# An attention and SwiGLU kernel: query loads one batch ahead, and the crossbar transpose at the first gate slot

## The chip, the cores and the metric

One core of a Trainium2 chip runs the kernel. The time is the device time of one execution in microseconds (us), as a median of several runs. The engines are TensorE (PE, with its weight loads as PEld), VectorE (DVE), ScalarE (ACT), GpSimd (POOL) and SyncE (SP). POOL and SP serve here as queues that issue DMAs, and each issues in the order in which the program writes them.

## The reference

Eight batches with eight heads, 576 tokens and 64 columns per head. Each head first pools its keys and values over the tokens into 32 memory slots, then attends to those; the result of all heads is the input of a gated feed-forward block.

```python
def _attn_ref(q, k, v, phi):
    a = np.exp(phi - np.max(phi, axis=2, keepdims=True))
    a = a / (np.sum(a, axis=2, keepdims=True) + 1e-09)
    k_m = np.einsum('bhsm,bhsd->bhmd', a, k)
    v_m = np.einsum('bhsm,bhsd->bhmd', a, v)
    scores = np.matmul(q, k_m.transpose(0, 1, 3, 2)) / np.sqrt(64)
    attn = np.exp(scores - np.max(scores, axis=-1, keepdims=True))
    attn = attn / (np.sum(attn, axis=-1, keepdims=True) + 1e-09)
    return np.matmul(attn, v_m)

def _moe_ref(x, w_gate, w_val, w_out):     # x: 4608 x 512, d_ff 1536
    g = x @ w_gate
    return (g * (1.0 / (1.0 + np.exp(-g))) * (x @ w_val)) @ w_out
```

## The kernel before

Everything is multiplied in bf16. The program is one straight list of instructions, and each engine runs its own part of the list in the written order; a manual schedule keeps that order. Waits between engines are semaphores that the framework sets from the data and from the reuse of buffers.

**Loads.** POOL issues all loads but the first phi: per batch phi (`load_phi`), keys and values into one tile t_kv (`load_k`, `load_v`), and the query t_q (`load_q`). The pool `inp` has two buffers for each of these tiles. So a load waits until the tile of two batches before has been read, and whatever stands behind it on POOL waits too. Since POOL has little else to do, it runs ahead of the code around it until such a wait stops it.

**The query's transpose.** The scores need the query with its 64 columns on the partitions (t_qT). In batches 0 and 1 TensorE makes it (`q_T`); from batch 2 on `load_qT` issues a DMA from SP that transposes t_q through the crossbar (L88). The same SP queue stores the output tiles (L410). t_qT has two buffers.

**One batch.** The exponential of phi (`phi_exp`, ScalarE); the sums over tokens of keys and values and their normalization (`kv_items`, tiles p_kv, t_bk, t_bv); a transpose of these on TensorE into t_kT (`kv_T`); the scores from t_kT and t_qT (`scores`, L274); their exponential; sums over the memory slots on TensorE and the inverse through a logarithm (`z_inv`, tile t_lz); and the normalized weights t_A on VectorE (`norm`, L303). The attention's output is never formed: the pooled values are multiplied with the gate and value weights (`u_round`, L316, tiles p_u, cast into t_U by VectorE or ScalarE; "vv" has both casts on VectorE, "av" one on each). Then each of 24 slots (`gv_slot`) multiplies t_A with t_U into a gate and a value (L349, p_g and p_v), ScalarE takes silu of the gate (L365, t_sg), and VectorE multiplies the two (L372, t_h).

**The output product** (`out_units`, L396, p_oo, from t_h and the output weights) needs two batches for its tiles of 128 tokens. Its products lie on a list, the backlog, and are taken from it to fill TensorE during the next batch: 28 of them between the scores and the first gate, the rest among the gate slots.

**What sets the order in a batch.** After the scores' stretch, written out by hand, `spread` merges several streams with the 24 gate slots: each stream has a list of items and a first and a last slot, and its items are spaced evenly between the two. So `(kvn, 9, 15)` puts the key/value sums of the next batch at slot 10.5 and the making of its t_kT at 13.5, and `(16, 17)` puts the transpose at slot 16.5.

Of the kernel before, what the change touches and what calls it, by code (L numbers as in the profile page):

```python
# [14 lines left out]
def kernel(  # L15
# [21 lines left out]
    B, H, S, D = q.shape  # L37
# [32 lines left out]
    def load_k(b):  # L70
        t = inp.tile([P, 2, H, J * D], BF16, tag="kv", name="t_kv")
        nc.gpsimd.dma_start(out=t[:, 0], in_=k[b].rearrange("h (p j) d -> p h (j d)", p=P))  # L72
        kvs[b] = t

    def load_v(b):
        nc.gpsimd.dma_start(
            out=kvs[b][:, 1], in_=v[b].rearrange("h (p j) d -> p h (j d)", p=P)
        )

    def load_q(b):  # L80
        t = inp.tile([P, H, J * D], BF16, tag="q", name="t_q")
        nc.gpsimd.dma_start(out=t, in_=q[b].rearrange("h (p j) d -> p h (j d)", p=P))  # L82
        qs[b] = t

    def load_qT(b):

        t = att.tile([128, H, 3, P], BF16, tag="qT", name="t_qT")
        nc.sync.dma_start_transpose(  # L88
            out=t.rearrange("p h j t -> p (h j) t"),
            in_=qs[b].rearrange("p h f -> p (h f)"),  # L90
        )
        for i in range(NP):
            qTs[b, i] = t[:, 2 * i:2 * i + 2].rearrange("p h j t -> p h (j t)")
# [48 lines left out]
    def kv_sum(b, p, parts):  # L142

        w0, w1 = parts[0], parts[-1] + 1
        n = (w1 - w0) * D
        for g in range(NG):
            for j in range(J):
                for i in range(NP):
                    nc.tensor.matmul(  # L149
                        p[32 * i:32 * i + 32, n * g:n * (g + 1)],  # L150
                        lhsT=ephis[b][:, j, g, i],
                        rhs=kvs[b][:, w0:w1, 2 * i + g, j * D:(j + 1) * D],
                        start=(j == 0),
                        stop=(j == J - 1),
                        tile_position=(0, 32 * i),
                    )

    def kv_denominators(b, p, o):
        for g in range(NG):
            for j in range(J):  # L160
                nc.tensor.matmul(  # L161
                    p[:, o + g:o + g + 1],
                    lhsT=ephis[b][:, j, g].rearrange("p i m -> p (i m)"),
                    rhs=ones1[0:P, :],
                    start=(j == 0),
                    stop=(j == J - 1),
                )
        r = att.tile([128, NG, 1, 1], FP32, tag="rS", name="t_rS")
        nc.vector.reciprocal(
            out=r.rearrange("p g a c -> p (g a c)"), in_=p[:, o:o + NG]  # L170
        )
        rSs[b] = r

    def k_norm(b, p):
        bk = att.tile([128, NG, 2, D], BF16, tag="bk", name="t_bk")
        nc.vector.tensor_tensor(
            out=bk,
            in0=p.to_broadcast([128, NG, 2, D]),
            in1=rSs[b].to_broadcast([128, NG, 2, D]),
            op=ALU.mult,  # L180
        )
        bks[b] = bk
# [11 lines left out]
    def kv_T(b, parts):  # L194
        p = ps.tile([128, 3, 128], BF16, tag="s", name="p_T")
        if 0 in parts:
            kTs[b] = att.tile([128, 3, 128], BF16, tag="kT", name="t_kT")
        if 1 in parts:
            nc.tensor.transpose(p[:, 2], bvs.pop(b).rearrange("p g d -> p (g d)"), ident)
        if 0 in parts:  # L200
            bk = bks.pop(b)
            for g in range(NG):
                nc.tensor.transpose(p[:, g], bk[:, g].rearrange("p a d -> p (a d)"), ident)
        lo, hi = (0 if 0 in parts else 2), (3 if 1 in parts else 2)
        nc.vector.tensor_copy(out=kTs[b][:, lo:hi], in_=p[:, lo:hi])
# [17 lines left out]
    def k_items(b):  # L223


        def sums():
            box["k"] = ps.tile([128, NG * D + NG], FP32, tag="s", name="p_kv")
            kv_sum(b, box["k"], (0,))

        def norm():  # L230
            kv_denominators(b, box["k"], NG * D)
            k_norm(b, box["k"][:, 0:NG * D].rearrange("p (g a d) -> p g a d", g=NG, a=1))

        return [sums, norm, lambda: kv_T(b, (0,))]
# [66 lines left out]
    def norm(b, g):  # L301
        a = att.tile([128, 2, HALF], BF16, tag=f"A{g}", name="t_A")
        nc.vector.tensor_tensor(out=a, in0=es.pop((b, g)), in1=lzs.pop((b, g)), op=ALU.mult)  # L303
        atts[b, g] = a
# [83 lines left out]
    def out_units(c, u, eng):  # L388

        mine = {}  # L390

        def unit(jf):
            def run():
                if jf == 0:
                    mine["p"] = ps.tile([128, DM], FP32, tag="o", name="p_oo")
                nc.tensor.matmul(  # L396
                    mine["p"],
                    lhsT=hts[c, jf][:, 128 * u:128 * (u + 1)],
                    rhs=WO[jf],
                    start=(jf == 0),  # L400
                    stop=(jf == NJF - 1),
                )
                if jf == NJF - 1:
                    t_o = work.tile([128, DM], FP32, tag="to", name="t_o")
                    if eng == "a":
                        nc.scalar.copy(out=t_o, in_=mine["p"])
                    else:
                        nc.vector.tensor_copy(out=t_o, in_=mine["p"])  # L408
                    for (r0, n, bb, jj, pp) in token_segments(2 * c * S + 128 * u, 128):
                        nc.sync.dma_start(  # L410
                            out=out_r[bb, jj, pp:pp + n, :], in_=t_o[r0:r0 + n, :]
                        )

            return run

        return [unit(jf) for jf in range(NJF)]

    def out_list(b):
        tiles = range(0, 4) if b % 2 == 0 else range(4, 9)
        res = []  # L420
        for n, u in enumerate(tiles):
            res += out_units(b // 2, u, "v" if n % 4 != 3 else "a")
        return res

    def q_items(b):
        return [lambda i=i: q_T(b, i) for i in range(NP)]

    def u_items(b, evac="av", tags=("ss",)):
        return [
            lambda c=c, which=which: u_round(  # L430
                b, which, c, evac, tags[(2 * c + which) % len(tags)]
            )
            for c in range(NCH)
            for which in range(2)
        ]

    def run(items):
        for x in items:
            x()
# [16 lines left out]
    def warm(n):  # L456

        p = ps.tile([128, DM], FP32, tag="o", name="p_oo")
        for _ in range(n):
            nc.tensor.matmul(p[:, 0:128], lhsT=bones, rhs=bones, start=True, stop=True)  # L460
# [59 lines left out]
    run(k_items(1)[:2])  # L520
    warm(8)
    run(q_items(1)[:2] + k_items(1)[2:] + q_items(1)[2:])
    load_k(2)
    load_v(2)
    load_q(2)
    u1v, u1 = u_items(1, "vv"), u_items(1)
    for g in range(NG):
        scores(1, g)
# [3 lines left out]
    nc.scalar.preload_act_table_set("silu_and_others")  # L532
    run(u1v[:1])
    norm(1, 0)
    run(u1v[1:2])
    norm(1, 1)
    backlog = out_list(0)

    def take(n):
# [5 lines left out]
    for b in range(1, B):  # L545
        last = b + 1 == B
        if b > 1:
            if not last:
                load_phi(b + 1, nc.gpsimd)
                load_k(b + 1)  # L550
                load_v(b + 1)
                load_q(b + 1)
            uw = u_items(b, "vv")
            exp_tables()
            run(take(2))
            for g in range(NG):
                scores(b, g)
            run(take(6) + uw[2:3] + take(4))
            if not last:
                phi_exp(b + 1)  # L560
            for g in range(NG):
                z_inv(b, g)
            nc.scalar.preload_act_table_set("silu_and_others")  # L563
            run(take(4) + uw[3:4] + take(4))
            norm(b, 0)
            norm(b, 1)
            run(take(8))
        rest = take(len(backlog)) if last else take(len(backlog) - 28)
        g = gv_slots(b)
        streams = [(g, 0, 24), (rest, 0, 24)]  # L570
        if b == 1:
            streams += [(u1[2:4], 1, 6), (u1[4:], 8, 14)]
        else:
            streams += [(u_items(b)[4:], 1, 8)]
        if not last:
            kvn = kv_items(b + 1)
            streams += [
                (kvn, 12, 17) if b == 1 else (kvn, 9, 15),
                ([lambda: load_qT(b + 1)], 16, 17),
                (u_items(b + 1)[:2], 18, 24),  # L580
            ]
        spread(*streams)
        flush_mul()
        backlog += out_list(b)
# [31 lines left out]
```

## Time and profile before

| | |
|---|---|
| Time, median of 3 runs | 292.21 us (290.81 to 294.08) |
| Time of the profiled execution | 294.86 us |
| Its span, first to last instruction | 293.0 us |
| TensorE busy | 254.7 us, 87% of the span |
| ScalarE, VectorE busy | 168.6 us, 165.9 us |
| GpSimd busy | 36.0 us |
| DMA: loads by POOL's queue, by SP's queue | 23.01 MB, 13.57 MB |

A matmul's end in the trace is modelled, and matmuls overlap, so a busy TensorE is not one at its peak. A row of a timeline gives start, duration, engine, line and operation, and in brackets the idle time of the engine before it and what ended that. The two queues are q0 (software, issued by POOL) and q1 (hardware, issued by SP).

### The profile page before, as it was taken

How to read it: one execution, taken by the hardware profiler on the slowest of the kernel's cores; microseconds unless marked ns; L12 is line 12 of the kernel's file. 1: busy time of each engine (PE TensorE's matmuls, PEld its weight loads, DVE VectorE, ACT ScalarE, POOL GpSimd, SP SyncE). 2: the span in 40 equal slices, each digit the busy share in tenths (PEclk: the TensorE clock that was granted, in tenths of full speed). 3: DMA queues.
4: the chain of work that ended last, by engine and by line, in shares of the span. 5: the costliest groups of instructions: out<-in, count | busy, mean ns of one | idle time of the engine just before them, and what ended most of it. 6: DMA issues, size and time to landing. Idle time of an engine off the chain costs nothing.

```text
span 293.0 us, 6428 instructions
## 1 busy us (share of the span) xinstructions
PE 254.7 (87%) x2504; PEld 148.6 (51%) x2538; DVE 165.9 (57%) x350; ACT 168.6 (58%) x354; POOL 36.0 (12%) x52
## 2 busy tenths in 40 slices
PE   7587997699439998599959999799999999999993
PEld 7552655356214565146733566346645664466541
DVE  0025785677406767167754677567867776666420
ACT  3148789565437647366557745785697457744300
POOL 8235523202011020100202020100000000000000
PEclk9655999799959999689997999999999999999999
DMA  7999999999979179572797439970512251211233
GB/s 153 225 196 196 219 204 205 207 219 211 209 72 226 36 108 152 90 167 74 92 187 148 124 65 167 104 153 22 115 40 74 54 102 38 72 38 36 73 97 84
DMA packets 48336, 37.00 MB, mean 126 GB/s; under 512 B 15921, under 2 KB 42801, under 8 KB 48305
## 3 DMA queue, kind: packets, MB, share of 16 engines
q0 software_dynamic: 27744, 23.01, 50.5%
q1 hardware_dynamic: 20560, 13.57, 22.6%
q8 instruction: 20, 0.33, 0.5%
q14 instruction: 12, 0.09, 0.1%
HBM read 42.47 MB, written 9.44 MB: 177 GB/s over the span
## 4 chain that ended last, share of the span: by engine, by line
PE 64%; DMA 23%; ACT 6%; DVE 3%; issue 2%; POOL 0%; ACTq 0%; POOLq 0%
PE p_oo L396 25%; DMA t_qT<-t_q 18%; PE p_g L349 15%; PE p_v L349 13%; PE p_u L316 5%; DMA t_q<-in_q_dram 4%; PE p_kv L149 2%; ACT t_lz L297 2%; PE p_g L274 1%; ACT L563 1%; DVE t_U L333 1%; ACT t_lz L298 1%; DVE t_A L303 1%; PE p_q L251 1%; PE p_kv L161 1%
## 5 line engine op out<-in xcount | busy, mean ns | idle before, releaser
L396 PE MATMUL p_oo<-WO,t_h 128*128 128x512 bf16 x398 | 119.6, 393 | 2.1 <-issue 1.0
L372 DVE TENSOR_TENSOR t_h<-t_sg,p_v 128x288 bf16<-128x288 bf16 x192 | 86.6, 454 | 45.7 <-PE p_v L349 42.1
L365 ACT ACTIVATE t_sg<-p_g 128x288 bf16<-128x288 f32 x192 | 79.0, 411 | 56.9 <-PE p_g L349 55.0
L349 PEld LDWEIGHTS <-t_U 128*128 128x128 bf16 x768 | 74.9, 99 | 44.8 <-issue 6.6
L349 PE MATMUL p_g<-t_A,t_U 128*128 128x288 bf16 x384 | 81.0, 292 | 5.9 <-DVE t_A L303 4.0
L349 PE MATMUL p_v<-t_A,t_U 128*128 128x288 bf16 x384 | 79.6, 291 | 0.1
L396 PEld LDWEIGHTS <-t_h 128*128 128x128 bf16 x432 | 41.7, 100 | 39.7 <-issue 15.7
L333 DVE CAST t_U<-p_u 128x512 bf16<-128x512 f32 (+1 forms) x70 | 42.9, 632 | 13.4 <-PE p_u L316 12.7
L408 DVE COPY t_o<-p_oo 128x512 f32<-128x512 f32 x28 | 19.3, 688 | 37.8 <-PE p_oo L396 37.6
L331 ACT CAST t_U<-p_u 128x512 bf16<-128x512 f32 (+1 forms) x38 | 20.1, 530 | 10.9 <-PE p_u L316 10.4
L316 PE MATMUL p_u<-W,t_kT 64*32 64x512 bf16 (+1 forms) x432 | 23.2, 381 | 1.6 <-DVE t_U L333 0.9
L274 PE MATMUL p_g<-t_qT,t_kT 64*32 64x288 bf16 x64 | 5.9, 359 | 17.5 <-DMA t_qT<-t_q 17.0
L135 ACT ACTIVATE t_ephi<-t_phi 96x768 bf16<-96x768 f32 x16 | 12.7, 846 | 9.7 <-DMA t_phi<-in_phi_dram 9.7
L316 PEld LDWEIGHTS <-t_kT 64*32 64x32 bf16 x432 | 6.6, 90 | 20.1 <-issue 19.0
L284 ACT ACTIVATE t_E<-p_g 128x288 bf16<-128x288 f32 x16 | 6.6, 414 | 16.9 <-PE p_v L274 16.9
L72 POOL DMA_DIRECT2D t_kv<-in_k_dram x8 | 6.3, 789 | 65.1 <-PE p_kv L149 47.2
L82 POOL DMA_DIRECT2D t_q<-in_q_dram x8 | 6.2, 773 | 60.0 <-DMA t_qT<-t_q 56.4
L274 PEld LDWEIGHTS <-t_kT 64*32 64x32 bf16 x128 | 1.7, 93 | 22.1 <-DMA t_qT<-t_q 19.0
L303 DVE TENSOR_TENSOR t_A<-t_E,t_lz 128x576 bf16<-128x576 bf16 x16 | 11.5, 750 | 1.0 <-ACT t_lz L298 1.0
L297 ACT ACTIVATE t_lz<-p_g 128x288 f32<-128x288 f32 x16 | 6.4, 402 | 8.9 <-PE p_g L294 8.8
L460 PE MATMUL p_oo<-bones 128*128 128x128 bf16 x98 | 10.0, 295 | 1.5 <-DVE bones L471 1.5
L298 ACT ACTIVATE t_lz<-t_lz 128x576 f32<-128x576 f32 x16 | 10.9, 684 | 0.5
(42 smaller groups left out, 138.4 us busy)
## 6 DMA issues: line engine op xcount, KB each, us to landing
t_kv<-in_k_dram POOLq DMA_DIRECT2D x8, 576.0 KB, 12.6
t_q<-in_q_dram POOLq DMA_DIRECT2D x8, 576.0 KB, 9.9
t_kv<-in_v_dram POOLq DMA_DIRECT2D x8, 576.0 KB, 15.7
out_dram<-t_o SPq DMA_DIRECT2D x24, 192.0 KB, 2.4
t_phi<-in_phi_dram POOLq DMA_DIRECT2D x7, 576.0 KB, 11.1
out_dram<-t_o SPq DMA_DIRECT2D x24, 128.0 KB, 2.4
W<-in_moe_w_gate_dram POOLq DMA_DIRECT2D x6, 256.0 KB, 13.1
W<-in_moe_w_val_dram POOLq DMA_DIRECT2D x6, 256.0 KB, 11.8
```

The source lines that it names most:

```text
L135: nc.scalar.activation(out=t[:, :, g].rearrange("p j i m -> p i j m"), in_=src[:, g], func=AF.Exp)
L297: nc.scalar.activation(out=lz[:, r], in_=p[r][:, 0:HALF], func=AF.Ln)
L298: nc.scalar.activation(out=lz, in_=lz, func=AF.Exp, scale=-1.0)
L303: nc.vector.tensor_tensor(out=a, in0=es.pop((b, g)), in1=lzs.pop((b, g)), op=ALU.mult)
L316: nc.tensor.matmul(p[g][32 * i:32 * i + 32, f0:f1], lhsT=kTs[b][64 * g:64 * g + 64, 2, 32 * i:32 * i + 32], rhs=w, start=True, stop=True, ...
L331: nc.scalar.copy(out=t[:, f0:f1], in_=p[g][:, f0:f1])
L333: nc.vector.tensor_copy(out=t[:, f0:f1], in_=p[g][:, f0:f1])
L349: nc.tensor.matmul(p[:, 0:HALF], lhsT=Us[b, which, c, g][:, 128 * o:128 * (o + 1)], rhs=atts[b, g][:, r], start=(g == 0), stop=(g == NG - 1),)
L365: nc.scalar.activation(out=sg, in_=gate, func=AF.Silu)
L372: nc.vector.tensor_tensor(out=dst, in0=sg, in1=val, op=ALU.mult)
L396: nc.tensor.matmul(mine["p"], lhsT=hts[c, jf][:, 128 * u:128 * (u + 1)], rhs=WO[jf], start=(jf == 0), stop=(jf == NJF - 1),)
L408: nc.vector.tensor_copy(out=t_o, in_=mine["p"])
```

## The change

Query loads move one batch ahead: before batch 1's slots, query 2 is loaded ahead of keys and values 2 and query 3 behind them, and batch b loads query b+2 in place of b+1. The transpose of the next batch's query is written at slot 0 (slot 6 in batch 1) in place of slot 16.5. In batch 1 the key/value sums of batch 2 move from slots 12 to 17 to slots 16 to 22, and the first U rounds of batch 2 from 18 to 24 to 21 to 24. Also in batch 1, the second U round comes behind both normalizations, with one of its casts on ScalarE.

```diff
+    load_q(2)
     load_k(2)
     load_v(2)
-    load_q(2)
+    load_q(3)
...
     run(u1v[:1])
     norm(1, 0)
-    run(u1v[1:2])
     norm(1, 1)
+    run(u1[1:2])
...
                 load_k(b + 1)
                 load_v(b + 1)
-                load_q(b + 1)
+                if b + 2 < B:
+                    load_q(b + 2)
...
             streams += [
-                (kvn, 12, 17) if b == 1 else (kvn, 9, 15),
-                ([lambda: load_qT(b + 1)], 16, 17),
-                (u_items(b + 1)[:2], 18, 24),
+                (kvn, 16, 22) if b == 1 else (kvn, 9, 15),
+                ([lambda: load_qT(b + 1)], 6, 6) if b == 1 else ([lambda: load_qT(b + 1)], 0, 0),
+                (u_items(b + 1)[:2], 21 if b == 1 else 18, 24),
             ]
```

On SP, from its first load on, before. The numbers are the program's buffer numbers: t_qT_1368 is batch 2's, t_qT_1886 batch 3's, and each t_o is one output tile.

```order
L67 DMA t_phi_84<-in_phi_dram 96x8x192
L410 DMA out_0_dram<-t_o_1328 96x512
L410 DMA out_0_dram<-t_o_1328 32x512
L88 DMA_TRANSPOSE t_qT_1368<-t_q_939 128x24x96
L410 DMA out_0_dram<-t_o_1509 64x512 x2
L410 DMA out_0_dram<-t_o_1560 32x512
L410 DMA out_0_dram<-t_o_1560 96x512
L410 DMA out_0_dram<-t_o_1595 96x512
L410 DMA out_0_dram<-t_o_1595 32x512
L410 DMA out_0_dram<-t_o_1722 64x512 x2
L88 DMA_TRANSPOSE t_qT_1886<-t_q_1476 128x24x96
```

The same place on SP after the change, where batch 2's is t_qT_1156 and batch 3's t_qT_1601.

```order
L67 DMA t_phi_84<-in_phi_dram 96x8x192
L88 DMA_TRANSPOSE t_qT_1156<-t_q_936 128x24x96
L410 DMA out_0_dram<-t_o_1265 96x512
L410 DMA out_0_dram<-t_o_1265 32x512
L410 DMA out_0_dram<-t_o_1511 64x512 x2
L410 DMA out_0_dram<-t_o_1562 32x512
L410 DMA out_0_dram<-t_o_1562 96x512
L410 DMA out_0_dram<-t_o_1597 96x512
L410 DMA out_0_dram<-t_o_1597 32x512
L88 DMA_TRANSPOSE t_qT_1601<-t_q_941 128x24x96
L410 DMA out_0_dram<-t_o_1726 64x512 x2
```

Batch 2's transpose now stands ahead of all stores, and batch 3's ahead of one more tile's store than before.

On POOL, from the last weights on, before: keys and values of batch 2, its query, then batch 3's phi, keys, values and query.

```order
L116 DMA WO2_132<-in_moe_w_out_dram 128x4x512
L72 DMA t_kv_936<-in_k_dram 96x8x384
L76 DMA t_kv_936<-in_v_dram 96x8x384
L82 DMA t_q_939<-in_q_dram 96x8x384
L67 DMA t_phi_1471<-in_phi_dram 96x8x192
L72 DMA t_kv_1473<-in_k_dram 96x8x384
L76 DMA t_kv_1473<-in_v_dram 96x8x384
L82 DMA t_q_1476<-in_q_dram 96x8x384
```

The same place on POOL after the change: t_q_936 is batch 2's query, t_q_941 batch 3's and t_q_1478 batch 4's.

```order
L116 DMA WO2_132<-in_moe_w_out_dram 128x4x512
L82 DMA t_q_936<-in_q_dram 96x8x384
L72 DMA t_kv_938<-in_k_dram 96x8x384
L76 DMA t_kv_938<-in_v_dram 96x8x384
L82 DMA t_q_941<-in_q_dram 96x8x384
L67 DMA t_phi_1473<-in_phi_dram 96x8x192
L72 DMA t_kv_1475<-in_k_dram 96x8x384
L76 DMA t_kv_1475<-in_v_dram 96x8x384
L82 DMA t_q_1478<-in_q_dram 96x8x384
```

One query load has come to stand ahead of keys and values 2; from there on the order of kinds is the same, with each query one batch further.

On VectorE, ahead of batch 1's first gate slots, before: casts of the first two U rounds (p_u) and the two normalizations (t_A).

```order
L333 CAST t_U_1048<-p_u0_1038 128x512
L333 CAST t_U_1050<-p_u1_1039 128x512
L303 TENSOR_TENSOR t_A_1052<-t_E_951,t_lz_1023 128x576
L333 CAST t_U_1064<-p_u0_1054 128x512
L333 CAST t_U_1066<-p_u1_1055 128x512
L303 TENSOR_TENSOR t_A_1068<-t_E_964,t_lz_1031 128x576
```

The same place on VectorE after the change.

```order
L333 CAST t_U_1050<-p_u0_1040 128x512
L333 CAST t_U_1052<-p_u1_1041 128x512
L303 TENSOR_TENSOR t_A_1054<-t_E_953,t_lz_1025 128x576
L303 TENSOR_TENSOR t_A_1056<-t_E_966,t_lz_1033 128x576
L333 CAST t_U_1070<-p_u1_1059 128x512
```

The second normalization stands ahead of the second round's cast; the other cast of that round is now on ScalarE, behind its table load.

## Rows read from the trace of the kernel before

**Rows 1.** The page's chain that ended last, by engine and by line.

```profile
PE 64%; DMA 23%; ACT 6%; DVE 3%; issue 2%; POOL 0%; ACTq 0%; POOLq 0%
PE p_oo L396 25%; DMA t_qT<-t_q 18%; PE p_g L349 15%; PE p_v L349 13%; PE p_u L316 5%; DMA t_q<-in_q_dram 4%; PE p_kv L149 2%; ACT t_lz L297 2%; PE p_g L274 1%; ACT L563 1%; DVE t_U L333 1%; ACT t_lz L298 1%; DVE t_A L303 1%; PE p_q L251 1%; PE p_kv L161 1%
```

**Rows 2.** The waits: who waited for what, total us, times, longest.

```profile
POOL t_q L82 <- DMA t_qT<-t_q: 56.4, 4, 16.4
...
PE p_g L274 <- DMA t_qT<-t_q: 17.0, 4, 8.3
```

**Rows 3.** Timeline of TensorE: the first scores of batches 2 to 5.

```profile
85.09 0.42 PE L274 MATMUL p_g<-t_qT,t_kT 64*32 64x288 bf16 x1 [8.28 <-DMA t_qT<-t_q]
...
120.49 0.42 PE L274 MATMUL p_g<-t_qT,t_kT 64*32 64x288 bf16 x1 [3.90 <-DMA t_qT<-t_q]
...
153.95 0.42 PE L274 MATMUL p_g<-t_qT,t_kT 64*32 64x288 bf16 x1 [3.26 <-DMA t_qT<-t_q]
...
186.80 0.29 PE L274 MATMUL p_g<-t_qT,t_kT 64*32 64x288 bf16 x1 [1.58 <-DMA t_qT<-t_q]
```

**Rows 4.** Two transposes in the chain (start, us), then the view of t_qT.

```profile
70.52 14.54 DMA t_qT<-t_q
...
105.01 15.44 DMA t_qT<-t_q
...
L88 SPq DMA_TRANSPOSE t_qT<-t_q x6: 2973/5584/8695, 70.5 to 232.5; - x6
...
DMA to landing us min/median/max: 5.0/11.6/15.4
```

**Rows 5.** DMA queues (packets, MB, share) at 52-54 us, 72-74 (q1), 76-78 (both).

```profile
q0 software_dynamic: 530, 0.40, 129.6%
...
q1 hardware_dynamic: 9, 0.02, 3.6%
...
q0 software_dynamic: 374, 0.28, 89.0%
q1 hardware_dynamic: 376, 0.10, 36.5%
```

**Rows 6.** First scores to first gate, batches 2 to 6; PEclk is third from the end.

```profile
85.09:94.31 9.22, 9.06 (x63) 3.50 (x65) 5.03 (x8) 6.75 (x14) 1.56 (x2) 0.81 0.85 177
120.49:130.50 10.01, 9.68 (x61) 3.63 (x63) 4.45 (x7) 6.74 (x14) 1.56 (x2) 0.71 0.74 144
153.95:162.93 8.98, 8.76 (x62) 3.49 (x64) 5.03 (x8) 6.74 (x14) 1.56 (x2) 0.83 0.84 170
186.80:194.18 7.38, 7.22 (x61) 3.16 (x63) 4.45 (x7) 6.74 (x14) 0.77 (x1) 1.00 0.82 132
214.30:222.14 7.84, 7.79 (x64) 3.34 (x65) 5.35 (x9) 7.53 (x15) 0.00 (x0) 1.00 0.28 69
```

**Rows 7.** DMA issues at 34-36 and 36.5-40 us: us to landing last.

```profile
t_kv<-in_k_dram POOLq DMA_DIRECT2D x1, 576.0 KB, 20.9
...
t_kv<-in_v_dram POOLq DMA_DIRECT2D x1, 576.0 KB, 21.3
```

**Rows 8.** Timeline of POOL: the issues of keys and values 2.

```profile
35.44 0.79 POOL L72 DMA_DIRECT2D t_kv<-in_k_dram  x1 [1.09 <-PE p_u L316]
37.98 0.78 POOL L76 DMA_DIRECT2D t_kv<-in_v_dram  x1 [1.74 <-DMA t_phi<-in_phi_dram]
```

**Rows 9.** TensorE's sums of batch 2; then from the view of p_T.

```profile
66.49 0.85 PE L149 MATMUL p_kv<-t_kv,t_ephi 96*32 96x128 bf16 x48 [0.38 <-ACT t_U L331]
...
PE p_u L316: 0.3, 1
```

**Rows 10.** Timelines of VectorE, ScalarE and TensorE ahead of batch 1's gates.

```profile
52.22 1.28 DVE L333 CAST t_U<-p_u 128x512 bf16<-128x512 f32 x2
...
52.37 1.28 ACT L532 ACT_TABLE_LOAD   x1
...
54.22 0.28 PE L349 MATMUL p_g<-t_A,t_U 128*128 128x288 bf16 x1 [1.58 <-DVE t_A L303]
```

## The prediction

> **What bounds the kernel now.** I read the chain that ended last first: TensorE holds 64% of it, DMA 23%, and the crossbar transpose that makes t_qT 18% [rows 1]. The waits say what of that is an idle TensorE: the scores at L274 wait for t_qT four times, 17.0 us in all, longest 8.3 [rows 2]. The timeline puts these waits at the first scores of batches 2, 3, 4 and 5: 8.28, 3.90, 3.26 and 1.58 us, together 17.02 [rows 3]; batches 6 and 7 have none. The transposes behind the first two were issued at 70.52 and 105.01 and took 14.54 and 15.44 us, while one with the queues empty lands in 5.0 [rows 4].
>
> Why they are slow is in the DMA packets. At 52 to 54 us the software queue, which carries all loads, moves 530 packets in 2 us; at 76 to 78, beside a transpose, it moves 374 and the transpose 376: the two queues share packet by packet [rows 5]. Before, a transpose is issued at slot 16.5 of a batch's 24, just after the key/value sums (slots 9 to 15, 12 to 17 in batch 1) have freed a buffer and so released the next keys and values. As long as there are loads left, it meets them, and only about 6 us of gate slots are left to hide it (TensorE ran out of work at 76.8 after the issue at 70.52).
>
> The idle time costs twice. From the first scores to the first gate, the granted clock averaged 0.81, 0.71 and 0.83 in batches 2, 3 and 4, so part of each stretch ran at the 1.2 GHz level; after the short wait of batch 5, and in batch 6 without one, it was 1.00 [rows 6]. Even and odd batches hold slightly different work here, so I compare 2 and 4 with 6, and 3 with 5: 9.22 - 7.84 = 1.38, 8.98 - 7.84 = 1.14, 10.01 - 7.38 = 2.63, together 5.15 us.
>
> **The transposes of batches 3 to 7** move from slot 16.5 to slot 0. On SP they now stand right behind the stores of the tiles that are copied out as the gates begin, so I expect them to issue about a microsecond after the first gate. From there to the next scores are 20 to 22 us: batch 2's first gate is at 85.09 + 9.22 = 94.31, and batch 3's scores could start at 120.49 - 3.90 = 116.59. Against 22.3 stands a worst landing of 15.44 [rows 4]. The source is there too: query b+1 is loaded behind the landing of transpose b-1, more than a batch before. The four waits fall to nothing: -17.02, with batch 2 included under the condition below. What hides the transposes is the gate slots; if that cover went, up to these 17 us would return. Stores on SP wait behind the transpose instruction (longest 8.7 us on SP [rows 4]); a tile is 12 of the 32 output products spread over 22.3 us, so one comes every 8 us, and there are three output buffers. I cost that at nothing; without that cover a copy would wait for what is left, at most 0.7 us a batch.
>
> **The clock**: without idle TensorE I take back the 5.15. The lower bound is 0, if the clock falls for another reason; the upper is 5.15, since the other stretches already show 1.00.
>
> **Batch 2 is the tight one.** Loads now stand on POOL as query 2, keys 2, values 2, query 3. Query 2 takes the place of keys 2, issued at 35.44 and landed 20.9 later, at 56.3 [rows 7, 8]; keys 2 take values' place (37.98 + 21.3 = 59.3), values 2 the query's, one load later again (62.3). The first transpose stands ahead of every store on SP, and its other waits are for batch 0's t_qT, long done, so it issues when query 2 lands, about 56.3, whatever slot the code names. Beside it the software queue still holds six loads of 3.0 us (the spacing of these landings): 18.0 us. In the same trouble at 70.52 the transpose took 14.54. Its 576 KB go in packets of some 256 bytes (0.10 MB in 376), 2,304 of them; at 376 per 2 us that is 12.3 us, and at 72 to 74 us only 9 had flowed [rows 5], so I add 3.5 for the start: 15.8. So it lands at 71 to 72; batch 2's scores could start at 85.09 - 8.28 = 76.8, 75.8 with the gain below. It holds by about 4 us.
>
> Keys and values 2 are read later, at slot 17.5 instead of 13.25. The old sums ran at 66.49 [rows 9], 12.3 us after the first gate at 54.22 [rows 10], so 0.93 us per slot; the new ones come at 70.4, against values that land at 62.3 plus 1 to 2 for the sharing. No wait. Then t_kT is copied one slot, not four, ahead of the first U round of batch 2, which must wait for the copy. The view of p_T has one such wait, 0.3 us [rows 9]. Bounds 0 to 1.0 (a copy queued behind one multiply); I take +0.3, nearest to the row.
>
> **The U round in batch 1.** VectorE runs two casts, 1.28 us from 52.22, between the two normalizations; the first gate waits 1.58 for the second [rows 10]. Now that second normalization can run when its t_lz is ready, at 52.37 where the table load begins, not at 53.50: 1.1 earlier. But one cast moves to ScalarE behind the 1.28 us table load, so it begins at 53.65 at the earliest, and the first value product and the first silu on ScalarE wait for it. Bounds 0 and -1.1; I take -0.7, as the gate comes 1.1 earlier and the value by somewhat less.
>
> **Sum** on the profiled execution (span 293.0, time 294.86): -17.02 - 5.15 - 0.7 + 0.3 = -22.6, giving 272.3. The median of the three runs shown is 292.21; from there it would be 269.6. If runs differ by these very waits, the first is the better basis; if by anything else, the second. I forecast **271.0**. What is late next is TensorE itself: undisturbed batches show it busy nearly throughout, 7.79 of 7.84 us [rows 6].
>
> **A rule against the clock term.** Batches 2 to 4 show 5.15 us, 1.8% of the span, going with low clocks [rows 6]. The Trainium skill (TensorE: Matmul & The Clock Gate, Part 1, "What's actually happening") says that "the ramp penalty is <1% of a typical kernel span". By that rule, an estimate from the page, at most 2.9 us would return and the sum would be about 274.5. The trace disagrees, so I leave the term whole. Rival C is the mechanism.
>
> **Rivals.**
> A, the forecast: waits and clock both go; 271.0, its own range 268 to 274. Chance 0.68.
>
> B, batch 2's transpose still late: the loads keep more than half of the engines, and the transpose ends only with the software queue. Then 56.3 + 18.0 + 5.0 = 79.3, against 75.8: a wait of 3.5 and a clock loss near batch 4's 1.14. 271.0 + 4.5 = 275.5. For: no transpose shown has met six loads. Against: the one-to-one packets give a fixed pace. 0.16.
>
> C, the clock stays low at the scores although nothing waits (odd batches did most poorly, for no visible reason): 271.0 + 2.6 to 5.15, say 274.5. Against: batches 5 to 7 at 1.00. 0.08.
>
> D, slower: the transposes and query loads close a loop. Transpose b+1 frees the buffer for query b+3, and POOL holds the next phi, keys and values behind that load. One turn is a transpose plus a query load: at the worst landings shown, 15.44 plus 21.3 [rows 4, 7], 36.7 us per two batches, against 57.6 of work (30.1 for an even batch: 7.84 plus 22.3; 27.5 for an odd one, from 186.80 to 214.30 [rows 6]). It decides only above 57.6; at 68 it would add 5.2 per batch, 26 over five, giving 297. 0.03.
>
> E, the change doesn't do what it says: SP reaches the transposes as late as before, because a store ahead waits for its tile. Then 17 us of waits stay: 292. Against: that tile is finished as the gates begin. 0.05.
>
> **How the numbers follow.** A measurement of this kernel tells about 1% from no change, 2.9 us. A, B and C are faster, 0.92; E the same, 0.05; D slower, 0.03. For 8 in 10 I take A's range and B and C: low 267.0 (269.6 less the rest of the U bound and some for the runs' spread), high 277.5 (B on the profiled basis: 272.3 + 4.5, rounded up).
>
> **What would show it.** Right: no wait of L274 for t_qT; granted clock 1.00 from first scores to first gate in batches 2 to 4; that stretch 7.4 (odd) or 7.8 (even); DMA out of the chain after 60 us; the first transpose issued at 56 and landing by 72; later ones landing in 5 to 8 us. Wrong: a wait at batch 2's scores (B); low clock without a wait (C); POOL holding keys past their slot (D); SP issues still late in the batch (E); or TensorE waiting for t_kT at the end of batch 1 by more than a microsecond.

## The result, and the profile after

The changed kernel takes 275.51 us (median of four runs, 272.71 to 276.99); the kernel before took 291.78 beside it (290.81 to 294.08). The ratio is 0.94, with a 95% interval of 0.930 to 0.950: faster, inside the range of 267.0 to 277.5, and 4.5 us above the 271.0 that stood for the likeliest case. The profiled execution is the longest of the four, 276.99 with a span of 275.2, so it is set against the sum's own basis of 272.3. Ratios here and below leave out executions more than 1.5% above the fastest of their kernel; the profiled one is just such a one, but `e2_q_pad`, profiled in an execution of 276.02 that is not left out, shows the same wait and the same granted clock at batch 2 (3.48 us, 0.73) and the same times in batches 3 and 4 (7.50, 7.84).

The page's chain of the changed kernel, by engine and by line, to be read beside [rows 1]:

```profile
PE 70%; DMA 13%; ACT 11%; issue 3%; DVE 1%; POOL 1%; ACTq 0%; POOLq 0%
PE p_oo L396 26%; PE p_g L349 17%; PE p_v L349 15%; DMA t_qT<-t_q 8%; PE p_u L316 5%; DMA t_q<-in_q_dram 4%; ACT t_lz L297 2%; PE p_kv L149 2%; ACT t_ephi L135 2%; ACT t_lz L298 2%; ACT L565 1%; ACT L451 1%; PE p_g L274 1%; ACT t_E L284 1%; PE p_q L251 1%
```

The transpose fell from 18% to 8% and did not leave. The waits say how often it still holds TensorE [rows 2]:

```profile
POOL t_q L82 <- DMA t_qT<-t_q: 93.2, 4, 28.3
...
PE p_g L274 <- DMA t_qT<-t_q: 3.5, 1, 3.5
```

One wait of 3.5 us in place of four with 17.0. In the timeline of TensorE, the first scores of batches 2 to 5 [rows 3]:

```profile
78.88 0.42 PE L274 MATMUL p_g<-t_qT,t_kT 64*32 64x288 bf16 x1 [3.55 <-DMA t_qT<-t_q]
...
111.20 0.29 PE L274 MATMUL p_g<-t_qT,t_kT 64*32 64x288 bf16 x1
...
138.82 0.29 PE L274 MATMUL p_g<-t_qT,t_kT 64*32 64x288 bf16 x1
...
168.87 0.29 PE L274 MATMUL p_g<-t_qT,t_kT 64*32 64x288 bf16 x1
```

Batches 3, 4 and 5 start without a wait; batch 2 waits 3.55. The windows from the first scores to the first gate, in the columns of [rows 6], with batch 2's idle time ahead of them:

```profile
75.33:78.88 3.55, 0.00 (x2) 0.00 (x1) 0.25 (x1) 0.83 (x1) 0.00 (x0) 0.81 0.96 172
78.88:88.98 10.10, 9.77 (x62) 3.69 (x64) 5.03 (x8) 6.74 (x14) 3.07 (x4) 0.73 1.00 183
111.20:118.70 7.50, 7.34 (x63) 3.22 (x63) 4.64 (x8) 7.40 (x15) 0.00 (x0) 1.00 0.51 98
138.82:146.66 7.84, 7.79 (x64) 3.33 (x65) 5.35 (x9) 7.52 (x15) 0.00 (x0) 1.00 0.93 177
168.87:176.37 7.50, 7.34 (x62) 3.24 (x63) 4.65 (x8) 7.39 (x15) 0.00 (x0) 1.00 0.14 39
```

Batches 3 to 5 run at the granted clock of 1.00 and take 7.50, 7.84 and 7.50 us, where they took 10.01, 8.98 and 7.38. Batch 2 is at 0.73 and takes 10.10, more than the 9.22 of before. The transposes, first batch 2's in the chain (start, us), then the view of t_qT [rows 4]:

```profile
55.63 23.20 DMA t_qT<-t_q
```

```profile
DMA to landing us min/median/max: 5.1/6.1/23.2
```

Batch 2's was issued at 55.63, as early as forecast, and landed 23.2 us later, at 78.83. The others land in 5.1 to 8.3. The DMA queues (packets, MB, share) at 62 to 72 us, then at 72 to 74 [rows 5]:

```profile
q0 software_dynamic: 975, 1.20, 91.9%
q1 hardware_dynamic: 982, 0.25, 46.1%
...
q0 software_dynamic: 354, 0.27, 90.4%
q1 hardware_dynamic: 345, 0.09, 38.6%
```

One packet against one holds in both. But at 62 to 72 the transpose gets 98 packets per us, not the 188 of [rows 5], and picks up again to 173 at 72. In the slow stretch a packet of the loads carries 1.20 MB / 975 = 1.23 KB on average, in the fast one 0.76 KB.

Stage by stage the 17.8 us that the span lost are: 1.5 up to batch 2's wait (half of it ahead of batch 1's first gate, where runs differ by about as much); 17.02 - 3.55 = 13.5 of waits; and 2.77 of the clock: 2.51 in batch 3 (10.01 to 7.50) and 1.14 in batch 4 (8.98 to 7.84), less the 0.88 that batch 2 lost (9.22 to 10.10).

### The profile page after: what moved, and what is told of

The parts are those of the page before. It is cut to its first block, busy times and chain, and to the rows that moved or that the text cites. A ratio compares the mean times of both kernels' runs of the same rounds, so it can differ in the third digit from the quotient of the medians.

```text
span 275.2 us, 6425 instructions
## 1 busy us (share of the span) xinstructions
PE 251.8 (91%) x2503; PEld 147.6 (54%) x2538; DVE 165.4 (60%) x349; ACT 168.8 (61%) x355; POOL 35.9 (13%) x52
## 3 DMA queue, kind: packets, MB, share of 16 engines
q1 hardware_dynamic: 20560, 13.57, 23.3%
## 4 chain that ended last, share of the span: by engine, by line
PE 70%; DMA 13%; ACT 11%; issue 3%; DVE 1%; POOL 1%; ACTq 0%; POOLq 0%
PE p_oo L396 26%; PE p_g L349 17%; PE p_v L349 15%; DMA t_qT<-t_q 8%; PE p_u L316 5%; DMA t_q<-in_q_dram 4%; ACT t_lz L297 2%; PE p_kv L149 2%; ACT t_ephi L135 2%; ACT t_lz L298 2%; ACT L565 1%; ACT L451 1%; PE p_g L274 1%; ACT t_E L284 1%; PE p_q L251 1%
## 5 line engine op out<-in xcount | busy, mean ns | idle before, releaser
L396 PE MATMUL p_oo<-WO,t_h 128*128 128x512 bf16 x397 | 117.0, 386 | 2.0 <-issue 0.8
L365 ACT ACTIVATE t_sg<-p_g 128x288 bf16<-128x288 f32 x192 | 78.8, 411 | 55.4 <-PE p_g L349 53.1
L333 DVE CAST t_U<-p_u 128x512 bf16<-128x512 f32 (+1 forms) x69 | 42.3, 631 | 10.8 <-PE p_u L316 10.1
L331 ACT CAST t_U<-p_u 128x512 bf16<-128x512 f32 (+1 forms) x39 | 20.7, 531 | 11.1 <-PE p_u L316 10.6
L316 PE MATMUL p_u<-W,t_kT 64*32 64x512 bf16 (+1 forms) x432 | 23.2, 379 | 1.5 <-DVE t_U L333 0.8
L82 POOL DMA_DIRECT2D t_q<-in_q_dram x8 | 6.2, 774 | 99.9 <-DMA t_qT<-t_q 93.2
L316 PEld LDWEIGHTS <-t_kT 64*32 64x32 bf16 x432 | 6.7, 90 | 19.5 <-issue 18.0
L406 ACT COPY t_o<-p_oo 128x512 f32<-128x512 f32 x8 | 4.7, 586 | 10.8 <-DMA out_dram<-t_o 10.0
L149 PE MATMUL p_kv<-t_kv,t_ephi 96*32 96x128 bf16 (+1 forms) x480 | 7.9, 219 | 2.8 <-DMA t_kv<-in_k_dram 2.8
L460 PEld LDWEIGHTS <-bones 128*128 128x128 bf16 x98 | 9.0, 135 | 1.5 <-DVE bones L471 1.5
```

What stands on the lines that cost most here:

```text
L149: nc.tensor.matmul(p[32 * i:32 * i + 32, n * g:n * (g + 1)], lhsT=ephis[b][:, j, g, i], rhs=kvs[b][:, w0:w1, 2 * i + g, j * D:(j + 1) * D] ...
L316: nc.tensor.matmul(p[g][32 * i:32 * i + 32, f0:f1], lhsT=kTs[b][64 * g:64 * g + 64, 2, 32 * i:32 * i + 32], rhs=w, start=True, stop=True, ...
L331: nc.scalar.copy(out=t[:, f0:f1], in_=p[g][:, f0:f1])
L333: nc.vector.tensor_copy(out=t[:, f0:f1], in_=p[g][:, f0:f1])
L365: nc.scalar.activation(out=sg, in_=gate, func=AF.Silu)
L396: nc.tensor.matmul(mine["p"], lhsT=hts[c, jf][:, 128 * u:128 * (u + 1)], rhs=WO[jf], start=(jf == 0), stop=(jf == NJF - 1),)
```

## The experiments

Each kernel differs from the changed one by the edit shown. Times are medians of four executions. The median of the kernel before, run beside them, was 293.07 (`e1`, `e2`, `e4`, `e5`), 292.70 (`e3`, `e6`, `e7`), 291.68 (`e8`, `e9`) and 293.10 (`e10`).

### Which half took away the waits of batches 3 to 5

The prediction gave the gain to the new slot (S); the rival is the earlier load of the query (L). `e4_slot_old` keeps the loads and puts the transposes back:

```diff
-                ([lambda: load_qT(b + 1)], 6, 6) if b == 1 else ([lambda: load_qT(b + 1)], 0, 0),
+                ([lambda: load_qT(b + 1)], 16, 17),
```

> The changed kernel with the transposes back at slot 16.5, query loads still one batch ahead. Theory S (the slot carries the gain): the transposes meet the next keys and values again, and batches 3 to 5 wait some 2 to 4 us each; with the clock 12 us come back on top of batch 2's, time near 285. Theory L (the loads carry it): a query load that waits for the transpose now stands ahead of the next phi, keys and values, so those cannot start before the transpose has landed; it runs alone, lands in 5 to 6 us inside the 7 us of slots left, and batches 3 to 5 do not wait; only batch 2 waits, 4 to 6 us, time 276 to 278.

271.98 us, ratio 0.9393 (0.9274 to 0.9512), so not slower than the whole change (0.94, 0.930 to 0.950). The timeline of TensorE at batch 2's scores, then of POOL in batch 3:

```profile
76.49 0.29 PE L274 MATMUL p_g<-t_qT,t_kT 64*32 64x288 bf16 x1 [2.58 <-DMA t_qT<-t_q]
```

```profile
101.27 0.77 POOL L82 DMA_DIRECT2D t_q<-in_q_dram  x1 [21.17 <-DMA t_qT<-t_q]
102.03 0.79 POOL L67 DMA_DIRECT2D t_phi<-in_phi_dram  x1
102.80 0.78 POOL L72 DMA_DIRECT2D t_kv<-in_k_dram  x1
```

Batches 3 and 5 to 7 don't wait, batch 4 waits 0.21. The reason stands on POOL: the query load needs the buffer that the transpose is reading, so it waits 21.17 us for it, and phi, keys and values are queued behind it. Batch 3's transpose, issued at 94.86, therefore runs without loads beside it and lands in 5.8 us. The order of the loads alone keeps them out of its way.

`e5_loads_old` keeps the new slots and puts the loads back:

```diff
-    load_q(2)
     load_k(2)
     load_v(2)
-    load_q(3)
+    load_q(2)
...
-                if b + 2 < B:
-                    load_q(b + 2)
+                load_q(b + 1)
```

> The changed kernel with the loads in the old order (keys, values, query of the same batch), transposes still at slot 0 (6 in batch 1). Theory S: batches 3 to 5 do not wait, since the query is there a batch ahead anyway and 20 us of slots are left; landings 5 to 9 us. Theory L: without the early loads the waits of batches 3 to 5 return, some 9 us and the clock, near 285. Batch 2 by both: query 2 lands three microseconds later per load ahead of it, near 62, and the transpose then meets phi, keys, values and query 3, so that it lands near 80 and the scores wait 4 to 6 us; time by theory S 276 to 278.

282.03 us, ratio 0.9751 (0.9617 to 0.9885): slower than the whole change, and whether it gains 2% on the kernel before is not settled. TensorE at batch 2's scores, and the view of t_qT:

```profile
85.08 0.42 PE L274 MATMUL p_g<-t_qT,t_kT 64*32 64x288 bf16 x1 [10.34 <-DMA t_qT<-t_q]
```

```profile
DMA to landing us min/median/max: 5.0/5.4/22.9
```

Batches 3 to 7 don't wait here either. So each half is enough for batches 3 to 5, and the two gains don't add. Batch 2 tells them apart: without the early query its transpose is issued at 62.18 instead of 55.63 and lands at 85.0, a wait of 10.34. What the change gained in batch 2 is the load order's. The early slot gains nothing there: with the old loads the transpose is issued 8.3 us earlier than before and lands at the same 85.0; with the new loads it lands at 78.8 from the new slot, and at 76.4 from the old one (66.08, 10.4 us to landing). Counted from batch 1's first gate, since runs start apart by a microsecond or two, the new slot's landings come at 34.0 us against 32.7 with the old loads, and at 27.2 against 25.9 with the new ones; each is one profiled execution.

### What slows batch 2's transpose: the query's packets?

The first guess was query 3, which the change had put into the queue. `e1_q3_behind` loads it behind phi, keys and values 3:

```diff
-    load_q(3)
...
                     load_q(b + 2)
+                if b == 2:
+                    load_q(3)
```

> The changed kernel with one load moved: query 3 goes behind phi, keys and values 3 instead of ahead of them. Batch 2's transpose still starts beside six loads (keys and values 2; phi, keys, values 3; query 3), but query 3 is now the last of them. Theory P (packet size): the two queues take turns packet by packet, and a query load consists of a few large packets, so beside it the transpose falls to half its pace; without it the pace stays near 376 packets in 2 us, it lands 15 to 18 us after its issue at about 55.6, near 72, the 3.55 us wait at batch 2's scores goes, the clock of that stretch returns to 1.00 and the stretch from 10.0 to about 7.8; time about 5.5 us less than the changed kernel, near 270. Theory W (sum of work): the transpose ends only with the software queue whatever stands in it; it lands near 79 again and the time stays near 275.

272.45 us, ratio 0.9429 (0.9238 to 0.962); the transpose lands in 20.9 us and the wait is 1.55. The large packets did not move with query 3: they now flow at 58 to 64 us, just before phi 3 lands (issued at 41.75, landed at 65.2), while query 3 at the end of the queue goes in small ones. `e2_q_pad` pads the query's tile, so that its rows don't lie end to end:

```diff
-        t = inp.tile([P, H, J * D], BF16, tag="q", name="t_q")
+        t = inp.tile([P, H + 1, J * D], BF16, tag="q", name="t_q")[:, 0:H]
```

> The changed kernel with the query tile one head wider than needed, so that the rows of a query load are no longer one closed block per partition; order of all loads unchanged, one head of each t_q tile is never written or read. Theory P: if that breaks the query's packets into the 768-byte pieces of the other loads (mean packet size of the software queue near 0.75 KB throughout 60 to 74 us, where it was 1.2 KB between 62 and 72), the transpose of batch 2 keeps 376 packets in 2 us and lands near 72; time near 270. If the packets stay large, nothing changes, 275, and this says nothing. Theory W: 275 in both cases, the landing near 79.

276.24 us, ratio 0.9542 (0.9418 to 0.9667); landing in 22.1 us, a wait of 3.48: nothing changed. The guess fell. Phi is the load that remains, and the only one that doesn't cast: f32 in memory and f32 in its tile.

### Phi's packets, or the whole queue?

Rival B of the prediction said that the transpose ends only with the software queue (W). `e6_phi3_first` loads phi 3 ahead of query 2, so that it is through before the transpose:

```diff
+    load_phi(3, nc.gpsimd)
     load_q(2)
...
-                load_phi(b + 1, nc.gpsimd)
+                if b > 2:
+                    load_phi(b + 1, nc.gpsimd)
```

> The changed kernel with the load of phi 3 moved ahead of query 2. The last runs put the slow stretch of batch 2's transpose where phi 3 flows: with phi 3 in its old place behind query 3 at 62 to 71 us, with query 3 put last still at 58 to 64. Theory P2 (the large packets are those of the phi loads, and the transpose gets one 256-byte packet per phi packet): phi 3 now flows before query 2 has landed, so the transpose never meets it; it is issued some 3 us later, near 58.5, keeps 376 packets in 2 us, takes 15 to 17 us, lands near 74.5 and batch 2's scores wait 0 to 0.5 us; time near 270.5. Theory W (it waits for the whole queue): the same six loads less one beside it, 58.5 + 15 + 5 = 78.5, a wait of 3 us, time near 275.

271.23 us, ratio 0.9296 (0.9217 to 0.9375). Batch 2's transpose in the chain, and the queues at 62 to 72 us:

```profile
57.90 17.78 DMA t_qT<-t_q
```

```profile
q0 software_dynamic: 1722, 1.29, 88.9%
q1 hardware_dynamic: 1740, 0.45, 40.8%
```

The loads move as many bytes as before (1.29 MB against 1.20), in 1,722 packets in place of 975, and the transpose gets 1,740 in place of 982. It lands at 75.7 although it starts 2.3 us later. A wait of 2.30 is left, where 0 to 0.5 was expected: the landing came 1.2 us later than expected, and TensorE was there at 73.4, in the changed kernel at 75.3. `e7_phi_pad` was meant to make phi's packets small by padding its tile:

```diff
-        t = inp.tile([P, H, J * M], FP32, tag="phi", name="t_phi")
+        t = inp.tile([P, H, J * M + 8], FP32, tag="phi", name="t_phi")[:, :, 0:J * M]
```

> The changed kernel with the phi tile 32 bytes longer per head and partition, so that the eight heads of a partition are no longer one closed block; order of all instructions unchanged, the added columns are never written or read. Theory P2: the phi loads go in 768-byte packets like the others (mean of the software queue 0.75 KB throughout 60 to 72 us), the transpose of batch 2 keeps 376 packets in 2 us and lands 15 to 17 us after its issue at 55.6, near 71.5; no wait, the stretch after it at clock 1.00 and 7.8 us; time 5.5 us below the changed kernel, near 270. Theory W: the landing stays near 79 and the time near 275. If the packets of phi stay large this says nothing.

276.34 us, ratio 0.9438 (0.9355 to 0.9521), a wait of 5.31. The transpose lands at 78.4, as in the changed kernel; the wait is longer because TensorE is there earlier, at 73.1. Its queues at 62 to 72 us:

```profile
q0 software_dynamic: 1086, 1.27, 91.3%
q1 hardware_dynamic: 1085, 0.28, 44.2%
```

The packets stayed large (1.17 KB on average), so the edit did not make what it should have tested. `e9_phi3_cast` does: phi 3 gets a bf16 tile, and its load casts as the others do and writes half the bytes in all.

```diff
-        t = inp.tile([P, H, J * M], FP32, tag="phi", name="t_phi")
+        if b == 3:
+            t = inp.tile([P, H, J * M], BF16, tag="phib", bufs=1, name="t_phi")
+        else:
+            t = inp.tile([P, H, J * M], FP32, tag="phi", name="t_phi")
```

> The changed kernel with one edit: the tile of phi 3 is bf16 in a buffer of its own, so its load casts as those of query, keys and values do; phi of that one batch is rounded to bf16, and its load writes half the bytes. Nothing moves in any order. P: between 60 and 72 us the software queue shows no packets over about 800 bytes, the pace stays at 185 to 190 per us, the transpose issued near 55.6 lands at 71 to 73, no wait for t_qT at batch 2's scores, granted clock 1.00 from first scores to first gate, 269 to 270.5. N: the transpose lands at 78 to 79 as before, a wait of 3 us or more, 275.

269.62 us, ratio 0.9292 (0.9225 to 0.9359). The queues at 62 to 72 us, and batch 2's first scores (L277 is L274 here, three lines lower):

```profile
q0 software_dynamic: 2083, 1.27, 88.4%
q1 hardware_dynamic: 2080, 0.53, 44.4%
```

```profile
75.99 0.29 PE L277 MATMUL p_g<-t_qT,t_kT 64*32 64x288 bf16 x1
```

No instruction moved in its engine's order, the loads write as many bytes in this stretch (1.27 MB), and only their packets are smaller, 0.61 KB on average. The transpose gets 208 packets per us, more than twice as many, lands in 17.5 us, and the wait is gone. The stretch behind it is at 1.00, 7.84 us.

`e8_phi3_last` puts phi 3 behind keys and values 3:

```diff
-                load_phi(b + 1, nc.gpsimd)
+                if b > 2:
+                    load_phi(b + 1, nc.gpsimd)
                 load_k(b + 1)
                 load_v(b + 1)
+                if b == 2:
+                    load_phi(b + 1, nc.gpsimd)
```

> The changed kernel with one edit: the load of phi 3 stands behind keys and values 3, not ahead of them. The same loads are still queued when batch 2's transpose is issued, but the ones beside it are all loads that cast. P (the transpose gets one packet per packet of its neighbour, and phi's packets are large): the pace stays at 185 to 190 packets per us from 60 us on, so the transpose, issued near 55.6, lands at 71 to 74, and the scores of batch 2 don't wait for t_qT. Phi 3 then lands last, at 79 to 81, some 2 to 3 us after ScalarE wants it, so a part of the gain may go to the waits behind its exponential; 270 to 273. N (what counts is how much is queued, whatever its packets): landing at 78 to 79, a wait of 3 us or more, 275.

272.82 us, the median of six executions, one of which took 413.33; ratio 0.9284 (0.9204 to 0.9364). The queues at 68 to 70 us and at 70 to 72:

```profile
q0 software_dynamic: 378, 0.29, 90.8%
q1 hardware_dynamic: 377, 0.10, 36.3%
...
q0 software_dynamic: 269, 0.36, 92.9%
q1 hardware_dynamic: 271, 0.07, 32.7%
```

The pace was 189 per us up to 70, as expected; then, with the transpose not yet done, packets of 1.34 KB on average appeared, and it fell. The landing took 21.0 us and the wait was 2.40. Phi 3 held ScalarE for 0.30 only. The expected landing was missed because I had phi's packets come behind the transpose; the pace before and after 70 answers to the packets again.

### The U round in batch 1

`e3_u_old` puts the second U round back between the normalizations, with both casts on VectorE:

```diff
     norm(1, 0)
+    run(u1v[1:2])
     norm(1, 1)
-    run(u1[1:2])
```

> The changed kernel with the second U round of batch 1 back ahead of the second normalization, both casts on VectorE. The prediction's term of 0.7 us: the first gate of batch 1 waits about 1.6 us for the second normalization instead of 0.56, and the stretch from the first gate to batch 2's last slot is 0.3 to 1.0 us longer. Since the transpose of batch 2 is the last to come there, a later batch 1 only shortens the wait for it (3.55 to about 2.8), so the time stays at 275 to 276. Rival: the cast on ScalarE costs as much as it saves, and the stretch is as long as in the changed kernel.

274.73 us, ratio 0.9392 (0.9313 to 0.9471), not to be told from the changed kernel. TensorE at the second half of the first gate:

```profile
52.17 0.39 PE L349 MATMUL p_g<-t_A,t_U 128*128 128x288 bf16 x1 [1.58 <-DVE t_A L303]
```

The wait of 1.58 is back; in the changed kernel it is 0.56. That is 1.0 us at this place. From batch 1's first gate to batch 2's scores, without the wait there, TensorE took 24.19 us against 23.71, so half a microsecond of it is left; with batch 2's transpose late (a wait of 3.67 here) none of it shows in the time.

### A better order

`e10_q2_ahead` loads query 2 ahead of the output weights:

```diff
-    for c in range(3):
-        load_wo(c)
...
     load_q(2)
+    for c in range(3):
+        load_wo(c)
     load_k(2)
```

> The changed kernel with one edit: the three loads of the output weights stand behind query 2, not ahead of it. Phi 3 keeps its large packets and its place. Query 2 is issued near 31 in place of 34.7 and lands near 52, so the transpose is issued near 52, 3.6 us earlier than in the changed kernel, and has that much longer beside packets of loads that cast. If the pace beside phi 3's packets is the whole matter, it has done 3.6 x 188 = 680 more of its 2,304 packets before phi's arrive, and lands at 73 to 75: no wait or at most 0.5 us at batch 2's scores, 269.5 to 271. If the transpose can't end before the software queue has emptied, it still lands near 78, with a wait of 3 us, 275. Against it: the last output weights land 3 us later, near 54, and the first output product runs at 52.6 today; at most 1 us for that.

270.21 us, each of four executions between 269.73 and 270.50 (beside 293.10 of before, with no ratio on record; the changed kernel's lie between 272.71 and 276.99). Batch 2's first scores, and the view of t_qT:

```profile
73.91 0.29 PE L274 MATMUL p_g<-t_qT,t_kT 64*32 64x288 bf16 x1
```

```profile
DMA to landing us min/median/max: 5.1/6.1/18.4
```

Query 2 landed at 47.3, the transpose 18.4 us later at 65.7, 8 us before its scores; I had it at 73 to 75. It was through before all but a few of phi 3's packets came (at 66 to 68 us the software queue moved 0.55 MB in 244 packets, 2.3 KB each), and long before the queue was empty: values 3, issued at 50.04, landed 26.8 us later, at 76.8. That speaks against W a second time. The output weights caused no wait. Of the kernels that do not round phi, this has the lowest median, though the 271.23 of `e6_phi3_first` can't be told from it.

## Why the prediction was right and where it failed

**The waits of batches 3 to 5** went, as forecast: 3.90 + 3.26 + 1.58 = 8.74 us. The reason given, the slot, is one of two that suffice (`e4_slot_old`, `e5_loads_old`).

**Batch 2** is the step that failed: "at 376 per 2 us that is 12.3 us ... So it lands at 71 to 72". The issue was right (56.3 against 55.63) and the share of one packet to one was right. The start was nearly right (3.5 allowed; some 44 packets had flowed 4.4 us after the issue), by luck in part: the 9 packets that it was read from [rows 5] carry 0.02 MB, 2 KB each, so they were the output stores', not the transpose's of 256 bytes. The pace was wrong. It was read from a stretch in which the neighbours were loads that cast, with 0.75 KB to a packet, and taken for all six loads. Phi 3 is one of the six; beside it the pace is 98 per us and the transpose takes 23.2 us instead of 15.8. Of these 7.4 us, an estimate from the packet counts puts 4.8 on the pace at 62 to 72 us (10 - 982/188), 0.6 on the start and 0.9 on the microsecond at 75, when the queues stood nearly still (the last section); the rest is not accounted for. A wait of 3.55 is left of 8.28.

**Rival B** named the case that came: landing at 79.3 (78.83), a wait of 3.5 (3.55), 275.5 us (275.51). That 275.51 lies inside the stated range is owed to the upper end, which was set for B; the forecast's own case ended at 274. B's mechanism was not the one: the transpose does not wait for the software queue to end (`e10_q2_ahead`; in the changed kernel itself values 3, issued at 50.39, landed 30.4 us later, at 80.8, 2 us behind the transpose), and with the same loads queued, phi 3's at half its bytes, it lands in time (`e9_phi3_cast`, at 74.5; half a load less is only 1.5 us by B's 3.0 us a load). The agreement to a tenth is chance. The point that the prediction set against B, "the one-to-one packets give a fixed pace", is the same error: the ratio is fixed, the pace isn't.

**The clock** gave 2.77 of the 5.15. Batches 3 and 4 returned nearly all of their terms (2.51 of 2.63, 1.14 of 1.14). Batch 2 should have returned 1.38 and took another 0.88. `e6_phi3_first`, `e4_slot_old` and `e9_phi3_cast` have this stretch at 1.00 and 7.6 to 7.8 us, so the term as such holds and hangs on the wait. The two batches alone return 3.65 us, 1.2% of the span of before. The prediction had set against this the sentence of the Trainium skill (TensorE: Matmul & The Clock Gate, Part 1, "What's actually happening") that "the ramp penalty is <1% of a typical kernel span"; it stands there for the first matmuls of a run, so it was not a rule for idle times in mid kernel, and the trace shows more than it here.

**The U round** gave 1.0 at the gate against 0.7; **t_kT** cost nothing that shows, against 0.3. TensorE's work from batch 1's first gate to batch 2's scores took 23.71 us against 24.45, so 0.7 for the two together against 0.4; `e3_u_old` (24.19) puts 0.5 of it on the U round.

**The sum** was -22.6 and came out at -17.9: 3.5 less of waits, 2.4 less of clock, 1.1 more in batch 1 and ahead of it. With the failed step mended by an experiment, the forecast's own case appears: 269.62 and 270.21 without a wait at batch 2's scores (`e9_phi3_cast`, `e10_q2_ahead`), and 271.23 with 2.30 of it left (`e6_phi3_first`).

**Rivals C, D and E** did not come: no low clock in batches 3 to 5, POOL holds the loads behind the query load (93.2 us of waits, up from 56.4) with no batch late for it, and SP issued the transposes at 55.63 and 90.48, the second 1.5 us after batch 2's first gate.

## What to carry to other kernels

When two DMA queues share engines, do not price a transfer by bytes or by a pace read elsewhere: here it got one packet for each packet of its neighbour, and fewer per microsecond beside large ones. Ask of each load that will be in flight how large its packets are, and keep a load with large ones away from a transfer of many small ones. Where a load feeds a DMA that feeds TensorE, move its place in the queue first; the slot of the second DMA matters only for what it then meets. And test the two halves of such a change apart: here each was enough for three of the batches, and in the fourth the traces show one of them delaying the landing by 1.3 us.

## What the runs showed that I had not expected

**Packets.** At 62 to 72 us, in six kernels, the software queue moved 1.20 to 1.30 MB each time, in 975, 1,086, 1,127, 1,722, 2,083 and 1,113 packets (the changed kernel, `e7_phi_pad`, `e2_q_pad`, `e6_phi3_first`, `e9_phi3_cast`, `e3_u_old`); the transpose's queue had 982, 1,085, 1,127, 1,740, 2,080 and 1,112. The Trainium skill (DMA: Bandwidth & Descriptors, "Queues, rings and completion order") says that an engine takes turns between its queues packet by packet; the trace agrees. That the load of phi, which doesn't cast, goes in the large packets follows from moving it (`e6_phi3_first`) and from making it cast (`e9_phi3_cast`). The traces also show it directly, by the sizes of packets at 62 to 72 us in the changed kernel and in `e9_phi3_cast`:

```profile
DMA packets 1957, 1.45 MB, mean 145 GB/s; under 512 B 1017, under 2 KB 1832, under 8 KB 1957
...
DMA packets 4163, 1.80 MB, mean 180 GB/s; under 512 B 2889, under 2 KB 4163, under 8 KB 4163
```

125 packets of the changed kernel are over 2 KB, none with phi 3 cast. The records of single packets give 4,608 bytes for each of them, six rows of 768, and 128 make up a load of phi; query, keys and values go in 768 packets of 768 bytes, and phi 3 when it casts in 768 of 384. `e7_phi_pad` has the same 4,608; why padding did not change that is open. It fits `e4_slot_old`, too: all but one of phi 3's packets had flowed when its transpose was issued at 66.08.

**Turns are not the whole of it.** Beside phi's packets each turn also took longer. By an estimate from the shares of the queues at 62 to 72 us (share x 16 engines x 10 us / packets), a packet of the transpose took 75 ns on average in the changed kernel, against 38 in `e6_phi3_first` and 34 in `e9_phi3_cast`, with the same 256 bytes. Why is open.

**The clock after an idle TensorE** doesn't follow the length of the wait alone. At batch 2's scores, waits of 1.55, 2.30 and 2.58 us left the stretch behind at 1.00, one of 2.40 had 0.82, those of 3.48, 3.55, 3.67, 5.31 and 10.34 us had 0.73, 0.73, 0.81, 0.72 and 0.73. So 10 us of idle time cost no more clock than 3.5. What decides at 2.4 was not tried. Batch 1 has such a loss without a wait for t_qT: from its first gate to where batch 2's scores could start, `e6_phi3_first` and `e7_phi_pad` took 22.14 and 22.15 us at a granted clock of 1.00, the ten other traces 23.3 to 24.5 at 0.93. What makes the difference was not tried. As it is about 1.5 us, the wait at batch 2's scores says less than the landing of the transpose.

**A gap of about 1 us in all DMA** stands beside batch 2's transpose: in the changed kernel at 75 to 76 only 17 and 21 packets flowed in the two queues, against 178 and 208 in the microsecond behind it. In `e1_q3_behind`, `e3_u_old`, `e6_phi3_first` and `e7_phi_pad` one microsecond between 71 and 74 has 34 to 77 packets in each queue, against 158 to 185 in the one ahead of it. `e10_q2_ahead` has one at 53 to 54 (45 in each), before any packet of phi 3, so it does not need them. Its cause stays open.
